# Moving the loads, the q turn and the last stores of a linear-attention and maxout-FFN kernel

## The chip, the cores and the metric

The kernel runs on one core of one Trainium2 chip. The metric is device time in microseconds (us) of a whole execution. The kernel before took 460.62 us (median of 2 runs, 459.97 to 461.27). All runs used here are in the fast state, and repeated runs of one kernel in one call agree within about 1%.

## The reference, cut to what matters

Batch 8, 8 heads, sequence 1024, head size 64. Keys and values are first projected along the sequence from 1024 to 64 rows, so attention is small; then a three-way maxout FFN (512 to 768 to 512) runs over all 8192 tokens.

```python
k_proj = np.einsum('ks,bhsd->bhkd', E, k)          # E, F: 64 x 1024
v_proj = np.einsum('ks,bhsd->bhkd', F, v)
scores = scale * np.matmul(q, k_proj.transpose(0, 1, 3, 2))
attn = softmax(scores)                             # (cut)
x = np.matmul(attn, v_proj)                        # -> (8192, 512)
h = np.maximum(np.maximum(x @ w1, x @ w2), x @ w3)
return h @ w_out
```

## The kernel before

All inputs are loaded by DMA issued from POOL (GpSimd), which casts to bf16 on the way (the page counts 57.15 MB read from HBM, the size of the inputs in float32; a load of 4 heads lands as 512 KB, its size in bf16). The main loop runs the FFN of batch b on TensorE and slips the attention of batch b+1 in between, in groups at "slots". A slot is one group of four or six FFN matmuls. Two operands must be turned (transposed): q into `qT`, and the projected k into `kpT`. In the main loop both turns are DMA transposes issued from SP. The score matmuls need both.

```python
def load(b, src, dst):                             # two DMAs of 4 heads each, from POOL
    ...
        nc.gpsimd.dma_start(out=dst[b % NB][:, hs], in_=sv[:, hs])

def q_turn(b):
    nc.sync.dma_start_transpose(out=qT[b % NB]..., in_=q_t[b % NB]...)

def attention(b, turn):                            # cut: the groups' bodies
    ...                                            # kv() ends its k part with turn(i), the k turn
    return [(2, kv), (10, lambda: scores(0)), (15, lambda: scores(1)), (20, sums),
            (25, lambda: av(0)), (30, lambda: av(1))]

def down(b, ch, c, tt):                            # second FFN layer, one 128-token tile
    ...
    nc.scalar.copy(out=o_acc[c % 2][:, tt, :], in_=ps[:, bank, :])
    if tt % 2 == 1:
        nc.gpsimd.dma_start(out=out_v[b, ch][:, tt - 1:tt + 1, :], in_=o_acc[c % 2][:, tt - 1:tt + 1, :])

load(1, k, k_t); load(1, v, v_t); load(1, q, q_t)
q_turn(1)
for b in range(B):                                 # "loop b" in the text
    groups = attention(b + 1, turn_dma) if b + 1 < B else []
    if b + 2 < B:
        load(b + 2, k, k_t); load(b + 2, v, v_t); load(b + 2, q, q_t)
    ...                                            # 36 l1 groups, 4 or 8 down groups; after each:
            while gi < len(groups) and groups[gi][0] <= slot:
                groups[gi][1](); gi += 1
            if slot == 16 and b + 2 < B:
                q_turn(b + 2)
```

`scores(0)` and `scores(1)` are the two halves of the score matmuls; `sums` makes the denominators of the softmax; `av` multiplies by the values and writes `xT`, the input of the next batch's FFN.

A load "at slot 9" does not start at a fixed time: POOL issues it when it has passed what stands before it in POOL's order.

The softmax here doesn't subtract the row's maximum and nothing guards it: scores larger than these inputs give would overflow.

Of the kernel before, what the change touches and what calls it, by code (L numbers as in the profile page):

```python
# [16 lines left out]
def kernel(ctx: ExitStack, tc: tile.TileContext, q, k, v, E, F, w1, w2, w3, w_out, out):  # L17
    nc = tc.nc
    B, H, S, D = q.shape
# [4 lines left out]
    DO = w_out.shape[1]  # L24
# [7 lines left out]
    def T(shape, dt, name):  # L32
        return sb.tile(shape, dt, name=name)

    ps = pp.tile([P, 8, 512], FP32, name="ps")
# [11 lines left out]
    NB = 2  # L47
    k_t = [T([P, H, SI, D], BF16, f"k_t{i}") for i in range(NB)]
    v_t = [T([P, H, SI, D], BF16, f"v_t{i}") for i in range(NB)]
    q_t = [T([P, H, SI, D], BF16, f"q_t{i}") for i in range(NB)]  # L50
    qT = [T([P, H, SI // 2, P], BF16, f"qT{i}") for i in range(NB)]
# [10 lines left out]
    o_acc = [T([P, SI // 2, DO], FP32, f"o_acc{i}") for i in range(2)]  # L62

    out_v = out.rearrange("(b p sp par) m -> b par p sp m", p=P, sp=SI // 2, par=2)
# [3 lines left out]
    def load(b, src, dst):  # L68
        sv = src[b].rearrange("h (p si) d -> p h si d", si=SI)
        for hh in range(2):  # L70
            hs = slice(hh * H // 2, (hh + 1) * H // 2)
            nc.gpsimd.dma_start(out=dst[b % NB][:, hs], in_=sv[:, hs])  # L72

    def q_turn(b):
        nc.sync.dma_start_transpose(
            out=qT[b % NB].rearrange("p h s t -> p (h s) t"),
            in_=q_t[b % NB].rearrange("p h si d -> p (h si d)"),
        )


# [71 lines left out]
    def fbank():  # L152
        state["f"] = (state["f"] + 1) % 4
        return state["f"]

    def l1(b, ch, c, jt, i):
        bank = fbank()
        for ct in range(NCT):
            nc.tensor.matmul(out=ps[:, bank, :], lhsT=w_sb[i][:, ct, jt * P:(jt + 1) * P],  # L159
                             rhs=xT[b % 3][:, ct, ch, :], start=(ct == 0), stop=(ct == NCT - 1))  # L160
        if i == 0:
            nc.scalar.copy(out=h1s[jt % 2], in_=ps[:, bank, :])  # L162
        elif i == 1:
            nc.vector.tensor_tensor(out=m12[jt % 2], in0=ps[:, bank, :], in1=h1s[jt % 2], op=ALU.max)  # L164
        else:
            nc.vector.tensor_tensor(out=hT[c % 2][:, jt, :], in0=ps[:, bank, :], in1=m12[jt % 2], op=ALU.max)  # L166

    def down(b, ch, c, tt):
        bank = fbank()
        for jt in range(NJT):  # L170
            nc.tensor.matmul(out=ps[:, bank, :], lhsT=hT[c % 2][:, jt, tt * P:(tt + 1) * P],  # L171
                             rhs=wo_sb[:, jt, :], start=(jt == 0), stop=(jt == NJT - 1))
        nc.scalar.copy(out=o_acc[c % 2][:, tt, :], in_=ps[:, bank, :])  # L173
        if tt % 2 == 1:
            nc.gpsimd.dma_start(out=out_v[b, ch][:, tt - 1:tt + 1, :], in_=o_acc[c % 2][:, tt - 1:tt + 1, :])  # L175


# [19 lines left out]
    for h in range(H):  # L197
        for s2 in range(SI // 2):
            nc.tensor.transpose(out=psb[:, h % 4, s2 * P:(s2 + 1) * P],  # L199
                                in_=q_t[0][:, h, 2 * s2:2 * s2 + 2, :].rearrange("p s d -> p (s d)"), identity=ident)  # L200
        (nc.vector.tensor_copy if h % 2 else nc.scalar.copy)(
            out=qT[0][:, h, :, :].rearrange("p s t -> p (s t)"), in_=psb[:, h % 4, 0:512])
# [2 lines left out]
    load(1, k, k_t)  # L205
    load(1, v, v_t)
    load(1, q, q_t)
    q_turn(1)

    pend = []  # L210
    for b in range(B):
        groups = attention(b + 1, turn_dma) if b + 1 < B else []
        if b + 2 < B:
            load(b + 2, k, k_t)
            load(b + 2, v, v_t)
            load(b + 2, q, q_t)
        slot = 0
        gi = 0

        def tick():  # L220
            nonlocal slot, gi
            slot += 1
            while gi < len(groups) and groups[gi][0] <= slot:
                groups[gi][1]()
                gi += 1
            if slot == 16 and b + 2 < B:
                q_turn(b + 2)

        for ch in range(2):
            c = 2 * b + ch  # L230
            for s in range(18):
                l1(b, ch, c, s // 3, s % 3)
                tick()
                if pend and s in (2, 5, 8, 11):
                    pend.pop(0)()
                    tick()
            pend = [lambda tt=tt, b=b, ch=ch, c=c: down(b, ch, c, tt) for tt in range(4)]
# [32 lines left out]
```

## Time and profile before

| what | value | view |
|---|---|---|
| span of the profiled run | 458.8 us | page |
| TensorE (PE) busy | 393.9 us, 86% | page, busy times |
| waits of score matmuls for kpT | 28.8 us in six waits | waits |
| k turn, from issue to landing (median) | 8.5 us | DMA view |
| granted TensorE clock, mean | 0.948 | cores view |

The page's picture of the span in 40 slices of 11.5 us. Each digit is a share in tenths; PEclk is the granted TensorE clock.

```profile
PE   1165903999899989999799989999899999999994
PEclk9995875999999998999899998999999999999998
DMA  7999999018961498029941697029921111111022
```

TensorE has a hole from 57 to 80 us (the sixth and seventh digits) and shallow dents about every four slices later. The DMA engines are full until 80 us and then work in bursts. The waits view of TensorE gives the cause (total us, times, longest us):

```profile
PE ps L110 <- DMA kpT<-kp: 28.8, 6, 17.4
PE ps L199 <- DMA q_t<-in_q_dram: 15.8, 2, 15.1
```

The second line is the start, before any data is there; no part of the change touches it. The first is the subject. SP's queue shows why kpT is late in loop 0 (start us, length us, what):

```profile
54.63 17.44 SPq L75 DMA_TRANSPOSE qT<-q_t  x1
72.12 1.65 SPq L141 DMA_TRANSPOSE kpT<-kp  x1
73.90 4.89 SPq L75 DMA_TRANSPOSE qT<-q_t  x1
113.89 1.19 SPq L141 DMA_TRANSPOSE kpT<-kp  x1
```

The q turn of batch 1 stands first and takes 17.44 us, the next one only 4.89. The k turn behind it goes out at 72.12, though its input was ready at 52.8, when the second copy of kp ended:

```profile
52.12 0.68 DVE L98 CAST kp<-ps 64x512 bf16<-64x512 f32 x1 [1.73 <-ACT kp L97]
```

The TensorE timeline has the price, a wait of 17.36 us; in loop 1 it is 2.21 us:

```profile
75.81 1.07 PE L110 MATMUL ps<-qT,kpT 64*64 64x512 bf16 x8 [17.36 <-DMA kpT<-kp]
...
122.58 0.63 PE L110 MATMUL ps<-qT,kpT 64*64 64x512 bf16 x8 [2.21 <-DMA kpT<-kp]
```

From one k turn to the next is one period of the loop. The view by stages, cut at the k turns (stretch, length, busy us of PE, PEld, DVE, ACT, POOL, then granted clock, DMA share, GB/s):

```profile
113.89:162.87 48.98, 46.77 (x274) 19.84 (x272) 22.14 (x30) 20.36 (x30) 7.37 (x10) 1.00 0.67 132
162.87:213.33 50.46, 48.45 (x274) 20.27 (x272) 22.13 (x30) 20.35 (x30) 7.36 (x10) 0.97 0.64 128
213.33:264.84 51.51, 48.46 (x274) 20.24 (x272) 22.14 (x30) 20.36 (x30) 7.35 (x10) 0.97 0.65 126
264.84:315.37 50.53, 48.43 (x274) 20.24 (x272) 22.14 (x30) 20.35 (x30) 7.36 (x10) 0.97 0.63 128
315.37:364.28 48.91, 46.78 (x274) 19.84 (x272) 22.13 (x30) 20.35 (x30) 2.88 (x4) 1.00 0.51 111
```

Every period contains a wait of 2.0 to 3.05 us. Three of the five also have 1.7 us more busy time for the same matmuls, at a mean clock of 0.97: stretches at half clock ("dips") follow those waits.

### The profile page before, as it was taken

To read this page: it belongs to the slowest core of one execution; us is meant where nothing else is said; L and a number is where in the kernel's file an instruction comes from. 1 tells how busy PE (TensorE), PEld (TensorE's weight loads), DVE (VectorE), ACT (ScalarE), POOL (GpSimd) and SP (SyncE) were. 2 spreads that over 40 slices of the span, in tenths; PEclk is the share of its full clock that TensorE was granted. 3 is DMA by queue.
4 is the path that set the end of the run, shared out by engine and by line. 5 is a ranking of instruction groups with operands and counts; after the bars stand their busy time and mean duration, and the time that the engine had idled before them with its cause. 6 is when DMAs were issued, how large, how long until landed. Compare 5 with 4: busy or idle time off the path is not lost.

```text
span 458.8 us, 5527 instructions
## 1 busy us (share of the span) xinstructions
PE 393.9 (86%) x2232; PEld 166.9 (36%) x2232; DVE 180.3 (39%) x248; ACT 166.5 (36%) x245; POOL 68.0 (15%) x101
## 2 busy tenths in 40 slices
PE   1165903999899989999799989999899999999994
PEld 0130301444344434344234433444344444444441
DVE  0022400464337432554137432644255435643440
ACT  1034201532463235522373234532552256223222
POOL 6163100004000400022000400031001000001001
PEclk9995875999999998999899998999999999999998
DMA  7999999018961498029941697029921111111022
GB/s 108 207 206 207 206 197 186 0 47 153 217 148 48 99 199 193 26 82 181 190 109 48 120 200 182 14 94 189 202 78 46 59 46 48 46 47 67 26 91 92
DMA packets 65353, 53.96 MB, mean 118 GB/s; under 512 B 34224, under 2 KB 61104, under 8 KB 65328
## 3 DMA queue, kind: packets, MB, share of 16 engines
q0 software_dynamic: 32624, 45.36, 48.3%
q1 hardware_dynamic: 32704, 8.26, 10.9%
q8 instruction: 17, 0.28, 0.2%
q14 instruction: 8, 0.07, 0.1%
HBM read 57.15 MB, written 16.78 MB: 161 GB/s over the span
## 4 chain that ended last, share of the span: by engine, by line
issue 79%; POOL 10%; DMA 9%; POOLq 0%
POOL out_dram L175 5%; DMA q_t<-in_q_dram 4%; DMA w_sb<-in_moe_w_dram 3%; DMA v_t<-in_v_dram 2%; POOL v_t L72 2%; POOL q_t L72 2%; POOL k_t L72 1%; POOL wo_sb L190 0%; POOLq L265 0%; POOL f_sb L180 0%; POOL e_sb L179 0%; POOLq L175 0%; POOL ident masks.py:199 0%; POOL ident masks.py:197 0%; POOLq L72 0%
## 5 line engine op out<-in xcount | busy, mean ns | idle before, releaser
L159 PE MATMUL ps<-xT,w_sb 128*128 128x512 bf16 x1152 | 267.8, 384 | 0.9 <-DVE xT L134 0.8
L159 PEld LDWEIGHTS <-w_sb 128*128 128x128 bf16 x1152 | 111.3, 99 | 146.8 <-issue 20.2
L164 DVE TENSOR_TENSOR m<-ps,h1s 128x512 f32<-128x512 f32 x96 | 66.2, 689 | 178.3 <-PE ps L159 149.4
L171 PE MATMUL ps<-wo_sb,hT 128*128 128x512 bf16 x384 | 96.6, 390 | 0.0
L162 ACT COPY h1s<-ps 128x512 f32<-128x512 f32 x96 | 56.1, 584 | 81.7 <-PE ps L159 81.3
L166 DVE TENSOR_TENSOR hT<-ps,m 128x512 bf16<-128x512 f32 x96 | 66.4, 692 | 28.8 <-PE ps L159 19.8
L173 ACT COPY o_acc<-ps 128x512 f32<-128x512 f32 x64 | 37.5, 586 | 110.6 <-PE ps L171 110.6
L175 POOL DMA_DIRECT2D out_dram<-o_acc x32 | 23.0, 718 | 358.5 <-ACT o_acc L173 333.4
L171 PEld LDWEIGHTS <-hT 128*128 128x128 bf16 x384 | 37.4, 100 | 50.2 <-issue 10.0
L113 ACT ACTIVATE pT<-ps 128x1024 bf16<-128x1024 f32 x32 | 30.9, 1022 | 44.7 <-PE ps L110 44.7
L134 DVE TENSOR_TENSOR xT<-ps,rinv 128x1024 bf16<-128x1024 f32 x32 | 37.6, 1216 | 18.2 <-PE ps L121 18.2
L110 PE MATMUL ps<-qT,kpT 64*64 64x512 bf16 x128 | 11.1, 417 | 31.0 <-DMA kpT<-kp 28.8
L199 PE MATMUL ps<-ident,q_t 128*128 128x128 bf16 x32 | 3.8, 312 | 15.8 <-DMA q_t<-in_q_dram 15.8
L129 ACT ACTIVATE rinv<-lns 128x1024 f32<-128x1024 f32 x16 | 16.9, 1056 | 0.5
L91 PE MATMUL ps<-k_t,eT 128*64 128x512 bf16 x64 | 17.0, 414 | 0.0
L93 PE MATMUL ps<-v_t,fT 128*64 128x512 bf16 x64 | 17.0, 413 | 0.0
L128 ACT ACTIVATE lns<-ps 128x1024 f32<-128x1024 f32 x16 | 16.2, 1014 | 2.0 <-PE ps L121 2.0
L110 PEld LDWEIGHTS <-kpT 64*64 64x64 bf16 x128 | 2.7, 108 | 38.3 <-DMA kpT<-kp 31.8
L121 PE MATMUL ps<-pT,vp 64*32 64x512 bf16 x256 | 12.0, 410 | 4.5 <-ACT lns L128 2.5
L72 POOL DMA_DIRECT2D k_t<-in_k_dram x16 | 12.2, 768 | 4.6 <-DMA wo_sb<-in_moe_w_out_dram 3.9
L72 POOL DMA_DIRECT2D q_t<-in_q_dram x16 | 12.2, 786 | 4.0 <-DMA v_t<-in_v_dram 3.6
L72 POOL DMA_DIRECT2D v_t<-in_v_dram x16 | 12.1, 772 | 3.6 <-DMA k_t<-in_k_dram 3.2
(33 smaller groups left out, 62.7 us busy)
## 6 DMA issues: line engine op xcount, KB each, us to landing
out_dram<-o_acc POOLq DMA_DIRECT2D x32, 512.0 KB, 3.2
k_t<-in_k_dram POOLq DMA_DIRECT2D x16, 512.0 KB, 8.5
v_t<-in_v_dram POOLq DMA_DIRECT2D x16, 512.0 KB, 13.3
q_t<-in_q_dram POOLq DMA_DIRECT2D x16, 512.0 KB, 16.9
w_sb<-in_moe_w_dram POOLq DMA_DIRECT2D x12, 192.0 KB, 9.7
wo_sb<-in_moe_w_out_dram POOLq DMA_DIRECT2D x1, 768.0 KB, 11.2
e_sb<-in_E_dram POOLq DMA_DIRECT2D x1, 128.0 KB, 3.2
f_sb<-in_F_dram POOLq DMA_DIRECT2D x1, 128.0 KB, 3.2
```

The lines of the kernel that those rows point to most:

```text
L72: nc.gpsimd.dma_start(out=dst[b % NB][:, hs], in_=sv[:, hs])
L91: nc.tensor.matmul(out=ps[0:KP, AB, :], lhsT=eT[:, si, :], rhs=k_t[i][:, :, si, :], start=(si == 0), stop=(si == SI - 1))
L93: nc.tensor.matmul(out=ps[KP:P, AB, :], lhsT=fT[:, si, :], rhs=v_t[i][:, :, si, :], start=(si == 0), stop=(si == SI - 1))
L113: nc.scalar.activation(out=pT[:, 2 * u + gg, :, :], in_=ps[:, AB + 2 * gg:AB + 2 * gg + 2, :], func=AF.Exp, scale=scale)
L134: nc.vector.tensor_tensor(out=xT[b % 3][:, 2 * u + half, :, :], in0=ps[:, AB + 2 * u:AB + 2 * u + 2, :], in1=rinv[u].rearrange("p (c n) -> ...
L159: nc.tensor.matmul(out=ps[:, bank, :], lhsT=w_sb[i][:, ct, jt * P:(jt + 1) * P], rhs=xT[b % 3][:, ct, ch, :], start=(ct == 0), stop=(ct == ...
L162: nc.scalar.copy(out=h1s[jt % 2], in_=ps[:, bank, :])
L164: nc.vector.tensor_tensor(out=m12[jt % 2], in0=ps[:, bank, :], in1=h1s[jt % 2], op=ALU.max)
L166: nc.vector.tensor_tensor(out=hT[c % 2][:, jt, :], in0=ps[:, bank, :], in1=m12[jt % 2], op=ALU.max)
L171: nc.tensor.matmul(out=ps[:, bank, :], lhsT=hT[c % 2][:, jt, tt * P:(tt + 1) * P], rhs=wo_sb[:, jt, :], start=(jt == 0), stop=(jt == NJT - 1))
L173: nc.scalar.copy(out=o_acc[c % 2][:, tt, :], in_=ps[:, bank, :])
L175: nc.gpsimd.dma_start(out=out_v[b, ch][:, tt - 1:tt + 1, :], in_=o_acc[c % 2][:, tt - 1:tt + 1, :])
```

## The change

The intent has three parts. In loops 1 to 5 the loads of batch b+2 are begun behind the k turn of b+1, with q first, and the q turn goes in two halves. In loop 0 the k turn goes ahead of the q turn, and the score groups are put off to slots 24 to 40. At the end the last stores leave POOL for the SP and ACT queues, and the last copy is split over two engines.

```diff
-    def q_turn(b):
+    def q_turn(b, hs):
         nc.sync.dma_start_transpose(
-            out=qT[b % NB]..., in_=q_t[b % NB]...
+            out=qT[b % NB][:, hs]..., in_=q_t[b % NB][:, hs]...
@@ down
-        nc.scalar.copy(out=o_acc[c % 2][:, tt, :], in_=ps[:, bank, :])
-        if tt % 2 == 1:
+        o = o_acc[c % 2]
+        if c == 2 * B - 1 and tt == 3:
+            half = DO // 2
+            nc.vector.tensor_copy(out=o[:, tt, :half], in_=ps[:, bank, :half])
+            nc.scalar.copy(out=o[:, tt, half:], in_=ps[:, bank, half:])
+            nc.sync.dma_start(out=out_v[b, ch][:, tt, :half], in_=o[:, tt, :half])
+            nc.scalar.dma_start(out=out_v[b, ch][:, tt, half:], in_=o[:, tt, half:])
+            return
+        nc.scalar.copy(out=o[:, tt, :], in_=ps[:, bank, :])
+        if c == 2 * B - 1:
+            nc.sync.dma_start(out=out_v[b, ch][:, tt, :], in_=o[:, tt, :])
+        elif tt % 2 == 1:
             nc.gpsimd.dma_start(...)
@@ main loop
-    q_turn(1)
...
-        if b + 2 < B:
-            load(b + 2, k, k_t)
-            load(b + 2, v, v_t)
-            load(b + 2, q, q_t)
+        if b == 0:
+            groups = [(at, g) for at, (_, g) in zip((2, 24, 28, 32, 36, 40), groups)]
...
-            if slot == 16 and b + 2 < B:
-                q_turn(b + 2)
+            if b == 0 and slot == 4:
+                q_turn(1, slice(0, H // 2))
+                q_turn(1, slice(H // 2, H))
+            if b + 2 < B:
+                if slot == 9:
+                    load(b + 2, q, q_t)
+                if slot == 11:
+                    load(b + 2, k, k_t)
+                    load(b + 2, v, v_t)
+                if slot == 18:
+                    q_turn(b + 2, slice(0, H // 2))
+                if slot == 27:
+                    q_turn(b + 2, slice(H // 2, H))
```

More of the change, by code (lines that the diff above doesn't have):

```diff
@@ L72, in load @@
             nc.gpsimd.dma_start(out=dst[b % NB][:, hs], in_=sv[:, hs])
-    def q_turn(b):
+    def q_turn(b, hs):
         nc.sync.dma_start_transpose(
-            out=qT[b % NB].rearrange("p h s t -> p (h s) t"),
-            in_=q_t[b % NB].rearrange("p h si d -> p (h si d)"),
+            out=qT[b % NB][:, hs].rearrange("p h s t -> p (h s) t"),
+            in_=q_t[b % NB][:, hs].rearrange("p h si d -> p (h si d)"),
         )
```

## The prediction

> **What bounds the kernel now.** TensorE: 393.9 of 458.8 us busy (the page). From the first FFN matmul (44.8 us) to the last (452.7) it stops for little but one thing: the waits view gives 28.8 us in six waits of the score matmuls for the transpose kpT. The TensorE timeline puts them at 58.5 (17.4 us, loop batch 0) and, in loops 1 to 5, just before the scores: 2.2, 2.0, 3.05, 2.1, 2.1 us. Loop 6, which loads nothing, waits 0. The view by stages shows a second cost: after the first wait the granted clock is 0.50 for 4.2 us, and after those of loops 2, 3, 4 it is 0.57 to 0.70 for about 4 us. Batches with a dip have 48.5 us of TensorE busy time, those without 46.8: 1.7 us each. [...]here gaps of 2.0 us were followed by a dip too.
>
> **Why kpT is late.** Loop 0: the q turn of batch 1 sits ahead of kpT in SP's queue and takes 17.44 us beside the loads (about 5 us later); kpT is issued only at 72.1, its input ready near 53.7. Loops 1 to 5: the loads of b+2 go out 8 us before kpT, which then takes about 8.5 us to land; in loop 6, without loads, 2.6. [...]
>
> **What the change does.**
> - Loops 1 to 5: the loads now stand in the POOL queue behind the output store of slot 8, which leaves about 5.7 us after kpT is issued. kpT lands in about 3 us on idle DMA engines, before slot 10. Removes 11.4 us of waits and three dips (5.1). q(b+2) is needed at slot 18, k and v a batch later: late loads cost nothing.
> - Loop 0: no store holds the POOL queue, so loads of batch 2 start as early as before. But kpT goes first, and scores are at slots 24 and 28. From 51.4 us, 90 matmuls of 0.216 us reach slot 24 near 70.8. Estimate: kpT and the two q halves, slowed as before, land near 60, 67 and 76. scores(0) needs the first half only: no wait; scores(1), near 75.3, waits 0 to 2 us. Removes 17.4 and the dip (2 us).
> - Added: the last AV group of batch 1 is at slot 40, the end of loop 0, so the next FFN waits for two multiplies of 1.18 us on VectorE behind a 0.69 us maximum: about 2.3 us, perhaps a dip.
> - Tail: last copy split over two engines (0.58 to about 0.35), last store 256 KB in halves instead of 512 KB after a POOL issue of 0.72 us: estimate 1.5 us saved.
>
> **Sum.** 460.6 - 17.4 - 2.0 - 11.4 - 5.1 - 1.5 + 2.3 + about 1 = 426.5 us. Nearly all is critical, as TensorE is busy throughout. Range 421 to 433. Faster by over 2%: 0.97; within 2%: 0.02; slower: 0.01.
>
> **Right or wrong by the profile.** Waits for kpT under 3 us in total; kpT to landing near 3 us in loops 1 to 6; granted clock near 1.00 in all loops after the first; batch periods of 46.8 us; a new wait of the FFN matmuls for xT near 92 us; last matmul to end of span 4.5 us instead of 6.1.
>
> **What would make it wrong.** q halves landing after 76 in loop 0; a clock dip at the loop 0/1 boundary or without any wait; loads meeting kpT after all; short stores on SP and ACT landing no faster.

(The 0.35 us of a half copy is the estimate; the nearest in the profile before are the copies of vp with 256 columns, 0.37 us on ACT and 0.43 us on VectorE. The 0.216 us of a matmul is the spacing in that profile: 12 FFN matmuls fill the 2.59 us from 95.16 to 97.75 us.)

## The result, and the profile after

The changed kernel took 430.89 us (median of 2 runs, 430.56 to 431.23), a ratio of 0.9355 (95% interval 0.929 to 0.942). A ratio here is the mean time of one kernel's runs over the mean of the other's runs of the same rounds, so it is not quite the ratio of the medians quoted. With 4 runs, it took 430.47 us, ratio 0.9361.

The slices of the page: the hole is a notch and the later dents are gone.

```profile
PE   1164897979999999999999999999999999999996
PEclk9985699898999999999999999999999999999999
DMA  7999999510799149931997169913996020111022
```

The waits view of TensorE: no wait for kpT is left. Two waits are new or larger, for qT and for xT.

```profile
PE ps L159 <- DVE xT L134: 4.0, 3, 2.1
PE ps L110 <- DMA qT<-q_t: 3.0, 1, 3.0
```

SP's queue, with the copy that feeds the k turn: the k turn goes out first, at 52.40, but the first half of the q turn alone occupies the queue for 9.93 us.

```profile
51.69 0.68 DVE L98 CAST kp<-ps 64x512 bf16<-64x512 f32 x1 [3.00 <-ACT kp L97]
...
52.40 1.28 SPq L141 DMA_TRANSPOSE kpT<-kp  x1
53.74 9.93 SPq L75 DMA_TRANSPOSE qT<-q_t  x1
...
103.53 1.19 SPq L141 DMA_TRANSPOSE kpT<-kp  x1
```

The TensorE timeline has the new waits: scores(0) in loop 0, and the first FFN matmuls of loop 1.

```profile
73.62 0.81 PE L110 MATMUL ps<-qT,kpT 64*64 64x512 bf16 x8 [3.04 <-DMA qT<-q_t]
...
96.28 0.59 PE L159 MATMUL ps<-xT,w_sb 128*128 128x512 bf16 x2 [2.15 <-DVE xT L134]
97.41 1.92 PE L159 MATMUL ps<-xT,w_sb 128*128 128x512 bf16 x5 [0.54 <-DVE xT L134]
```

The stages cut at the k turns again (two of five equal ones shown). The period is 46.70 us, clock 1.00.

```profile
103.53:150.23 46.70, 46.44 (x269) 19.84 (x272) 22.14 (x30) 20.35 (x30) 7.38 (x10) 1.00 0.73 139
150.23:196.93 46.70, 46.44 (x269) 19.84 (x272) 22.14 (x30) 20.36 (x30) 7.37 (x10) 1.00 0.74 138
```

Cutting both spans at the same places gives the whole account. The first cut is where the k turn of batch 1 could go out (52.83 before: 0.03 us after the copy of kp, as in the changed kernel) or went out (52.40 after).

| stretch | before, us | after, us | saved |
|---|---|---|---|
| start, to the first k turn ready | 52.83 | 52.40 | 0.4 |
| loop 0, to the second k turn | 61.06 | 51.13 | 9.9 |
| loops 1 to 5, to the last k turn | 250.39 | 233.48 | 16.9 |
| from there to the end | 94.52 | 92.49 | 2.0 |
| span | 458.8 | 429.5 | 29.3 |

The start is the same code up to small moves; in the other variants below that issue the k turn first, it went out between 51.35 and 53.21, so 0.4 us of the start is not evidence for anything. Loop 0 varies too: in the later profile of the same changed kernel (after_again) it took 49.13 us and not 51.13, without the half clock at its end.

### The profile page after: what moved, and what is told of

It reads as the page before. It is cut to its first block, busy times and chain, and to the rows that moved or that the text cites. A ratio compares the mean times of both kernels' runs of the same rounds, so it can differ in the third digit from the quotient of the medians.

```text
span 429.5 us, 5508 instructions
## 1 busy us (share of the span) xinstructions
PE 388.4 (90%) x2192; PEld 166.6 (39%) x2232; DVE 180.7 (42%) x249; ACT 166.4 (39%) x245; POOL 66.6 (16%) x99
## 4 chain that ended last, share of the span: by engine, by line
PE 82%; DMA 8%; ACT 3%; DVE 3%; issue 2%; POOL 1%; SPq 0%; DVEq 0%; ACTq 0%; POOLq 0%
PE ps L159 53%; PE ps L171 19%; DMA qT<-q_t 5%; PE ps L91 4%; DMA q_t<-in_q_dram 4%; PE ps L121 3%; PE ps L110 2%; DVE xT L134 1%; ACT lns L128 1%; ACT pT L113 1%; PE ps L93 1%; ACT rinv L129 0%; PE ps L209 0%; POOL k_t L72 0%; POOL v_t L72 0%
## 5 line engine op out<-in xcount | busy, mean ns | idle before, releaser
L159 PE MATMUL ps<-xT,w_sb 128*128 128x512 bf16 x1122 | 264.0, 382 | 5.7 <-DVE xT L134 4.0
L171 PE MATMUL ps<-wo_sb,hT 128*128 128x512 bf16 x374 | 92.9, 381 | 0.6
L166 DVE TENSOR_TENSOR hT<-ps,m 128x512 bf16<-128x512 f32 x96 | 66.4, 692 | 19.8 <-PE ps L159 10.7
L185 POOL DMA_DIRECT2D out_dram<-o_acc x30 | 21.5, 718 | 323.4 <-ACT o_acc L181 313.4
L91 PE MATMUL ps<-k_t,eT 128*64 128x512 bf16 x64 | 18.4, 437 | 0.0
L93 PE MATMUL ps<-v_t,fT 128*64 128x512 bf16 x64 | 18.1, 433 | 0.0
L129 ACT ACTIVATE rinv<-lns 128x1024 f32<-128x1024 f32 x16 | 16.9, 1057 | 0.5
L97 ACT CAST kp<-ps 64x512 bf16<-64x512 f32 x8 | 4.6, 578 | 21.5 <-PE ps L93 21.5
L98 DVE CAST kp<-ps 64x512 bf16<-64x512 f32 x8 | 5.5, 683 | 17.3 <-ACT kp L97 17.3
## 6 DMA issues: line engine op xcount, KB each, us to landing
v_t<-in_v_dram POOLq DMA_DIRECT2D x16, 512.0 KB, 17.4
```

Source lines behind the costliest of these rows:

```text
L91: nc.tensor.matmul(out=ps[0:KP, AB, :], lhsT=eT[:, si, :], rhs=k_t[i][:, :, si, :], start=(si == 0), stop=(si == SI - 1))
L93: nc.tensor.matmul(out=ps[KP:P, AB, :], lhsT=fT[:, si, :], rhs=v_t[i][:, :, si, :], start=(si == 0), stop=(si == SI - 1))
L159: nc.tensor.matmul(out=ps[:, bank, :], lhsT=w_sb[i][:, ct, jt * P:(jt + 1) * P], rhs=xT[b % 3][:, ct, ch, :], start=(ct == 0), stop=(ct == ...
L166: nc.vector.tensor_tensor(out=hT[c % 2][:, jt, :], in0=ps[:, bank, :], in1=m12[jt % 2], op=ALU.max)
L171: nc.tensor.matmul(out=ps[:, bank, :], lhsT=hT[c % 2][:, jt, tt * P:(tt + 1) * P], rhs=wo_sb[:, jt, :], start=(jt == 0), stop=(jt == NJT - 1))
```

## The experiments

All were correct and were timed in 3 rounds (4 runs each, 7 of the kernel before). "All" below means the changed kernel with only the stated edit undone or altered. They ran on three chips; the kernel before had medians of 460.85, 460.85 and 459.92 us.

| label | what | median us | ratio to before |
|---|---|---|---|
| e_tail | stores only | 457.75 | 0.9938 |
| e_loop0 | loop 0 only | 449.35 | 0.9749 |
| e_steady | loops 1 to 5 only | 442.28 | 0.9600 |
| e_oldload | all, loads at the loop's top | 448.16 | 0.9726 |
| e_whole | all, q turns whole | 432.78 | 0.9392 |
| e_order | all, old slots in loop 0 | 438.84 | 0.9545 |
| e_slots | all, q turn whole and ahead of k turn in loop 0 | 432.92 | 0.9413 |
| e_av | all, closer slots in loop 0 | 429.46 | 0.9298 |
| e_gate | all, loads of batch 2 held back | 425.57 | 0.9225 |
| e_gate_early | e_gate, and early slots | 421.87 | 0.9158 |
| after_again | all | 430.47 | 0.9361 |

### Do the three parts add up?

e_tail is the kernel before with only the new `down`; e_loop0 and e_steady take the main-loop part of the diff for `b == 0` alone and for `b > 0` alone (in e_loop0 the loads stay at the top of the loop, with q first for batch 2).

> Only the last stores changed. Theory: they save what the trace of the changed kernel shows from the issue of the last k turn to the end, 2.0 us, so ratio near 0.9957 and about 458.6 us. Rival: the 2.0 us there come from a warmer clock at the end and the stores give 0.5 us or less (459.9 or more). Last matmul to end of span should be 4.5 us against 6.1 before.

> Only loop 0 changed (k turn of batch 1 ahead of the q turn, q in halves, score groups at slots 24 to 40, loads of batch 2 with q first); later loops and stores as before. Theory: the gains add, and loop 0 gives about 10.4 us by the distance from the first to the second k turn: 450 us. Kept: five waits of about 2 us for kpT in loops 1 to 5. Rival: the loop-0 part moves the phase of the later loops, so that the clock dips there change in number (each 1.7 us) and the sum does not add up.

> Only loops 1 to 5 changed (loads at slots 9 and 11, q turns in halves at 18 and 27); loop 0 and stores as before. Theory: removes 11.4 us of waits for kpT and the three clock dips that followed them, 5.1 us: 444 us, batch period 46.7 us, clock 1.00 in loops 1 to 6. Rival for the dips: they have nothing to do with the waits, so they stay: 449 us, waits gone but 48.5 us of busy time in some batches.

By stages, starts left out, the parts add up: 2.1 us (e_tail, from the last k turn on), 10.0 (e_loop0, loop 0) and 16.9 (e_steady, loops 1 to 5) are 29.0, and the change saved 28.9. By ratio they do not quite: 0.6%, 2.5% and 4.0% are 7.1%, where the change gained 6.4% to 6.5%, some 3 us less, which is more than the intervals allow. The starts can do that: e_steady and e_tail have the same code up to there, and their kp was ready at 51.15 and at 53.42 us. In e_steady the wait for kpT in loops 1 to 5 and all three half-clock stretches went together, period 46.7 us, which is against the rival that the clock had nothing to do with the waits. In e_loop0 and e_tail the five waits stayed, and so did three half-clock stretches, in loops 2 to 4.

For the stores, the stretch from the last k turn to the end was 92.37 us in e_tail against 94.52 before, and 94.50 in e_loop0 with the old stores (mean clock there 0.99, 0.98 and 0.98). That is 2.1 us, against 2.0 expected. But by the trace the split copy had no part in it. The end of the timeline, before:

```profile
452.70 0.58 ACT L173 COPY o_acc<-ps 128x512 f32<-128x512 f32 x1 [0.71 <-PE ps L171]
453.58 0.72 POOL L175 DMA_DIRECT2D out_dram<-o_acc  x1 [1.88 <-ACT o_acc L173]
```

and after:

```profile
425.44 0.42 DVE L176 COPY o_acc<-ps 128x256 f32<-128x256 f32 x1 [4.49 <-PE ps L171]
425.89 0.33 SPq L178 DMA_DIRECT2D out_dram<-o_acc  x1
425.90 0.37 ACT L177 COPY o_acc<-ps 128x256 f32<-128x256 f32 x1 [1.17 <-DVE o_acc L176]
426.30 0.37 ACTq L179 DMA_DIRECT2D out_dram<-o_acc  x1
```

The two half copies ran one after the other: 0.83 us from the first start to the last end, against 0.58 for one whole copy. The trace puts ACT's wait of 1.17 us down to DVE's copy; both read one PSUM bank. Whether the shared bank is the reason for that wait, and whether the wait was needed, no run shows; the trace shows its price. What paid is the stores: issue 0.33 to 0.37 us and 1.8 to 1.9 us to landing (128 KB from SP and ACT), against 0.72 and 3.2 us (512 KB from POOL). Size and queue changed together, so which of the two did it stays open; no run has the new stores with a whole copy, either.

### Is it the place of the loads in loops 1 to 5?

```diff
@@ top of loop b
+        if b + 2 < B:
+            load(b + 2, q, q_t); load(b + 2, k, k_t); load(b + 2, v, v_t)
@@ slots
-                if slot == 9: load(b + 2, q, q_t)
-                if slot == 11: load(b + 2, k, k_t); load(b + 2, v, v_t)
```

> The changed kernel with the loads of b+2 back at the top of loop b (q still first, q turns still in halves at slots 18 and 27). Theory: the place of the loads is what counts; the waits for kpT in loops 1 to 5 come back with about 2 us each and some dips, kpT landing near 8.5 us: 441 to 448 us. Rival: the order (q first) or the halves took the waits away; then it stays near 431 us.

The waits for kpT came back, with 8.6 us (median) from issue to landing and periods of 48.6 to 51.5 us:

```profile
PE ps L110 <- DMA kpT<-kp: 11.9, 5, 3.1
```

It took 448.16 us, at the upper end of what was expected. So the place of the loads did it, and neither the order with q first nor the halves did. The DMA view of the kernel before and of the changed one shows the same for the k turn (count, median us to landing):

```profile
kpT<-kp SPq DMA_TRANSPOSE x7, 8.5
```

```profile
kpT<-kp SPq DMA_TRANSPOSE x7, 2.6
```

### What slows the q turn in loop 0?

e_whole puts the q turn in one piece again. e_gate holds the loads of batch 2 back until the q turn has landed:

```diff
+    gate = T([P, 1], BF16, "gate")
...
                 if slot == 9:
+                    if b == 0:   # POOL waits here for the end of the second q half
+                        nc.gpsimd.tensor_copy(out=gate, in_=qT[1][:, H - 1, SI // 2 - 1, 0:1])
                     load(b + 2, q, q_t)
```

> The changed kernel, with the loads of batch 2 held back in loop 0 until the q turn of batch 1 has landed (a one-column copy on POOL that reads the end of the second half goes ahead of them). Theory: beside a load stream the q turn hardly advances, in halves or not; without it kpT lands in about 2.6 us (now 8.1), the first q half in about 4 to 5 us (now 19.8), scores(0) does not wait (now 3.0 us) and the clock dip after it goes (1.7 us): about 426 us. The wait at the end of loop 0 for xT stays. Rival: the halves are slow for another reason (a cost of their own, about 10 us each); then scores(0) waits as now or longer, 431 us or more.

> The changed kernel with each q turn in one piece. Theory: the halves bring little, because the first one lands hardly before a whole one would (19.8 us after issue, in the kernel before 20.4 for the whole): scores(0) waits 1 to 2 us longer, 432 to 433 us. Rival (what was predicted: a half lands in half of the time): scores(0) would wait 6 us or more longer, 437 us or more.

e_gate took 425.57 us, as the theory said. The tile view of qT between 50 and 70 us of the changed kernel, and between 50 and 64 us of e_gate, has the time from issue to landing of the two halves:

```profile
DMA to landing us min/median/max: 11.6/15.7/19.8
```

```profile
DMA to landing us min/median/max: 4.6/4.7/4.8
```

Without the load stream a half lands in 4.7 us, not in 11.6 and 19.8, and scores(0) no longer waits. Cutting the DMA view to windows shows what each queue moved. In the kernel before, between 56 and 71 us, the loads (first line) moved 2.38 MB and the transposes (second line) 0.57 MB, in a similar number of packets (packets, MB, share of the engines):

```profile
q0 software_dynamic: 2403, 2.38, 93.9%
q1 hardware_dynamic: 2212, 0.57, 28.5%
```

In e_gate, between 54 and 59.4 us, with no load beside them, the transposes moved 1.04 MB:

```profile
q1 hardware_dynamic: 4136, 1.04, 104.2%
```

That is 0.57 MB / 15 us = 38 GB/s beside the loads, and 1.04 MB / 5.4 us = 193 GB/s alone. The packets have 990 and 258 bytes (bytes over packets). That the two counts are near each other over the whole window is in part chance: at its start the turn had only begun, at its end the loads ran out. In its middle third, 61 to 66 us, they are equal:

```profile
q0 software_dynamic: 779, 0.78, 91.2%
q1 hardware_dynamic: 780, 0.20, 29.9%
```

With as many packets as the loads, the transposes with their small packets moved a fifth of the bytes in this window (0.20 of 0.98 MB). How the engines share their time between queues, no run shows.

So the one 17.44 us turn was not slow all through: about half of it (0.57 of about 1.04 MB) crawled beside the loads until 71 us, and the rest had landed by 75.0 us (54.63 + 20.4), when the loads were over (0.05 MB between 71 and 79.5 us). Halving this turn did not halve the time to its first half. In the changed kernel the first half landed at 73.5 us and the second at 75.3 (issue 53.74 + 19.8, and 63.7 + 11.6); in e_whole the whole landed at 75.7 (53.45 + 22.2). The halves were worth 3.0 us of waiting (3.0 against 6.0 us) and about 2 us of time (432.78 us for e_whole; the changed kernel had 430.89 and 430.47. They were run at other times.). The theory had said 1 to 2 us of waiting, so it was low there; the rival's 6 us and more did not come either. In loops 1 to 5 the halves made no difference: the period of e_whole is 46.7 us too.

### Order or slots in loop 0?

e_order keeps the k turn first and sets the slots back to `(2, 10, 15, 20, 25, 30)`. e_slots keeps the late slots and calls `q_turn(1)` whole before the loop again.

> The changed kernel with the groups of loop 0 back at slots 2, 10, 15, 20, 25, 30 (k turn still ahead of the q turn). Theory: with the load stream beside it the first q half lands near 73.5 us whatever stands ahead of it, so scores(0), now reached near 58.5 us, waits about 13 to 15 us for qT instead of 17 us for kpT; the wait at the end of loop 0 goes: 437 to 441 us. Rival: putting the k turn first is what removed the wait of loop 0; then scores(0) waits under 5 us and it takes 432 us or less.

> The changed kernel with the q turn of batch 1 whole and ahead of its k turn again, as before the change, but the groups of loop 0 at the late slots. Theory: the late slots carry nearly all of the gain of loop 0: kpT lands near 75 us, scores(0) reached near 70.6 waits 4 to 5 us: 432 to 433 us. Rival: the order carries it: 440 us or more.

Both times came as the theory said. In e_order scores(0) waited 15.0 us, now for qT, and it took 438.84 us. In e_slots it waited 5.4 us for kpT (4 to 5 expected) and took 432.92, only 2.5 us more than after_again:

```profile
72.69 1.07 PE L110 MATMUL ps<-qT,kpT 64*64 64x512 bf16 x8 [15.02 <-DMA qT<-q_t]
```

```profile
75.52 1.07 PE L110 MATMUL ps<-qT,kpT 64*64 64x512 bf16 x8 [5.41 <-DMA kpT<-kp]
```

e_slots also has the q turn whole; e_whole, whole with the k turn first, took 432.78 us in another call, so at the late slots the order made no difference that can be seen. So putting off the scores carries the gain of loop 0. The reordering alone swaps a wait for kpT for one almost as long for qT.

### The end of loop 0, and a version that beats both

e_av uses the slots `(2, 24, 27, 30, 33, 36)`, so that the last attention group is not at the very end of loop 0. e_gate_early is e_gate with `(2, 12, 17, 22, 27, 32)`, since with the loads held back q is there early.

> The changed kernel with the groups of loop 0 at 24, 27, 30, 33, 36 instead of 24, 28, 32, 36, 40. Theory: the FFN of loop 1 no longer waits for xT (2.7 us) and its dip goes (1.7 us); closer groups cost up to 1.5 us of waits for the exponentials: 427 to 428 us. The wait of scores(0) for the q half (3.0 us) stays. Rival: the boundary cost less than it looks, or the waits between the closer groups give it all back: 430 us or more.

> As e_gate, and the groups of batch 1 in loop 0 at slots 12, 17, 22, 27, 32 instead of 24 to 40. Theory: with the q turn landed by about 61 us the late slots are not needed, and the wait of the next FFN for xT at the end of loop 0 (2.7 us) and the dip after it (1.7 us) go as well: about 422 us, faster than both kernels. Rival: q lands too late for slots 12 and 17 and scores wait 2 to 4 us: 424 to 428 us.

e_gate_early took 421.87 us, 8.4% less than the kernel before (ratio 0.9158; the changed kernel's is 0.9361, so it gains about 2% on that. It was run at another time.). Loop 0 there is free of large waits and at full clock (51.35:93.78, against 52.40:103.53 and clock 0.93 after):

```profile
51.35:93.78 42.43, 41.46 (x245) 17.48 (x248) 22.05 (x30) 17.93 (x26) 6.09 (x9) 1.00 0.90 155
```

e_av missed. The wait for xT at the end of loop 0 did go, but 429.46 us (one run of the four had 426.15) is only about 1 us better, not 3 to 4. In its profile scores(0) waited 3.9 us, the closer groups waited another 1.2 us for DVE, and the half clock after scores(0) lasted two grid windows instead of one. Set against the changed kernel's first profile, the wait for xT and the half clock after it (2.7 and 1.7 us) went; 0.9 us more of wait for q, 1.2 us for DVE and about 1 us of half clock (5.3 us of busy time in it against 3.4, half of that lost) came. That leaves 1.3 us by this sum; loop 0 became 1.0 us shorter (50.17 against 51.13).

### When does the clock drop?

> The changed kernel itself, to have it in the same rounds: 430 to 432 us. Theory on the clock dips: a 3.41 us window of the clock grid with less than about 1.45 us of TensorE busy time is followed by half clock; so the wait of scores(0) always gives a dip, the one at the end of loop 0 only where a window holds most of it.

What the traces show of this theory: reading the granted clock in 1 us windows over each of 13 traces (the kernel before, the changed one, and the eleven experiments) gives the times of its changes between 1.0 and 0.5. Within each trace they all fall on one grid of 3.413 us, up to a few hundredths: in the kernel before, for example, the changes at 49.5, 172.4 and 274.8 us are 36 and 30 steps apart. Cutting each trace on its own grid, from 41 us on to near the last matmul: every full-clock window with at most 1.44 us of TensorE busy time was followed by half clock, and every one with 1.48 us or more was not. (Busy times include the modelled ends of matmuls. Before 41 us, while data is still arriving, one window breaks the limit: in e_order the one at 25.62 us had 1.53 us and half clock followed. So the limit is not that sharp.) The two kinds in the kernel before, loop 1 and loop 2, each with the next grid window:

```profile
121.19:124.60 3.41, 2.02 (x15) 0.84 (x16) 0.38 (x1) 1.55 (x2) 0.00 (x0) 1.00 1.25 205
124.60:128.01 3.41, 3.41 (x21) 1.39 (x18) 1.00 (x2) 1.55 (x3) 0.00 (x0) 1.00 1.05 229
168.98:172.40 3.42, 1.42 (x13) 0.39 (x12) 0.69 (x1) 0.77 (x2) 0.29 (x1) 1.00 1.24 202
172.40:175.81 3.41, 3.41 (x10) 1.21 (x9) 0.69 (x1) 1.36 (x2) 0.00 (x0) 0.50 0.96 251
```

The wait of loop 1 was longer (2.2 us against 2.0) but a grid line cut it in two, so the two windows still had 2.60 and 2.02 us of work. The same limit tells apart two runs of the very same kernel. In the changed kernel's first profile the window at the end of loop 0 had 1.00 us busy and half clock followed; in after_again it had 1.61 us and none did:

```profile
94.41:97.82 3.41, 1.00 (x4) 0.38 (x4) 2.95 (x3) 0.00 (x0) 0.00 (x0) 1.00 0.00 0
97.82:101.23 3.41, 3.41 (x14) 1.18 (x14) 0.69 (x1) 0.58 (x1) 0.00 (x0) 0.50 0.00 0
```

```profile
95.47:98.88 3.41, 1.61 (x7) 0.57 (x6) 2.34 (x3) 0.59 (x1) 0.00 (x0) 1.00 0.00 0
98.88:102.29 3.41, 3.41 (x25) 1.52 (x24) 1.35 (x2) 0.58 (x1) 0.00 (x0) 1.00 0.00 0
```

No run was built to place a wait on the grid on purpose, so the limit separates what was seen from 41 us on; it is not a controlled test.

## Why the prediction was right or wrong, point by point

The range (421 to 433) held 430.89 us and the direction was right. The point, 426.5, was 4.4 us too low. Loop 0 alone fell 6.2 us short; small extra gains elsewhere gave part of it back.

| term | predicted saving | measured | by |
|---|---|---|---|
| loops 1 to 5: waits and half clock | 11.4 + 5.1 = 16.5 | 16.9 | stages; e_steady alone 18.6 |
| loop 0: waits, half clock, boundary | 17.4 + 2.0 - 2.3 - 1 = 16.1 | 9.9 | stages |
| stores | 1.5 | 2.0 | stages; e_tail |

- **Loops 1 to 5: right**, in mechanism and size. The k turn lands in 2.6 us, no wait is left, the clock stays at 1.00, and the period is 46.70 us (46.8 foreseen). e_oldload shows that the place of the loads did it. The late loads cost nothing, as foreseen.
- **Loop 0: right in direction, wrong in one step.** The step that failed is "kpT and the two q halves, slowed as before, land near 60, 67 and 76. scores(0) needs the first half only: no wait". It spread the 17.44 us evenly over the turn. In fact the turn ran at 38 GB/s beside the loads and fast only once they had ended (193 GB/s alone, in e_gate); kpT landed at 60.5 (52.40 + 8.1) as foreseen, the first half at 73.5 and not 67, and scores(0), reached at 70.6 (70.8 foreseen), waited 3.0 us. That wait also kept a stretch of half clock (0.50 from 73.94 to 77.35 us) that had been counted as removed. e_gate undid both by taking the loads away.
- **The boundary of loop 0: right in mechanism, 2.7 us against 2.3.** The half clock after it (1.7 us; "perhaps a dip" in the text, nothing in the sum) did come in the profiled run. With 2.0 us for the extra wait net of the 1 us allowed, 1.7 for each of two half-clock stretches and 0.4 for the boundary, 5.8 of the missing 6.2 us are named. In after_again the half clock at the boundary did not come, with 1.61 us busy in its grid window against 1.00, so by these two runs that part depends on where a run falls on the clock grid.
- **Half clock after waits: right that the waits cause it (both went together in e_steady), incomplete on when.** The prediction noted that 2.0 us had sufficed and had no reason why 2.2 had not; the grid gives one: by it the waits of 2.0 and 2.2 us left 1.42 and 2.02 us of work in their windows.
- **Stores: a little more than foreseen, but not by the split copy.** The copy was to shrink from 0.58 to 0.35 us; it took 0.83.

## What to carry to other kernels

Here a transpose in small packets beside a bulk load crawled until the load ended (38 against 193 GB/s). So move the load out of its way or hold it back by a dependency, rather than reorder or halve the transpose (e_gate took 425.57 us; e_order, which had the reordering without the late slots, 438.84, and halving gained about 2 us). Count a wait of TensorE by its length plus, where it left less than about 1.45 us of work in a 3.41 us clock window of these traces, the half-clock window that followed (1.7 us). Two engines that shared a last copy out of one PSUM bank went one after the other here (0.83 us against 0.58 for one whole copy), and the split bought nothing; whether two banks would have let them overlap, no run shows.
